# Attention and a mixture of experts on one core: late routing of one batch, a drain on GpSimd's queue, and one ScalarE copy moved forward

## The chip, the core and the metric

One core of a Trainium2 chip runs the whole program. Its engines are TensorE (PE), VectorE (DVE), ScalarE (ACT), GpSimd (POOL) and SyncE (SP), which only issues DMAs here. The metric is the device time of one execution in microseconds, as a median of several runs. PE does the matmuls; the other engines copy, split, rotate, reduce and issue transfers beside it.

## The reference, cut to what matters

The reference takes q, k, v of shape 8 x 8 x 576 x 64 (batch, heads, tokens, width) and computes an attention with rotary embedding, then a mixture of experts with one expert per token:

```python
q_rot, k_rot = rotate(q), rotate(k)
scores = q_rot @ k_rot^T / sqrt(64); attn = softmax(scores)
x = (attn @ v) as 4608 rows of 512                       # 8 batches of 576 rows
logits = x @ w_gate + modality_bias[modality_id]         # 8 experts
e = argmax(logits); gate = softmax(logits)[e]
out[rows of e] = gate * (relu(x[rows of e] @ w1[e]) @ w2[e])   # 512 -> 1024 -> 512
```

Which rows go to which expert is known only when the logits of all tokens are there, so the kernel has to sort rows by expert on the chip.

## The kernel before, in words

**Attention.** Two heads make a pair; there are 32 pairs, four for each batch of 576 tokens. Of every pair the program knows some sixty jobs by name: scores (S0 to S8), the row minimum on VectorE (MN), the exponential on ScalarE (EX), transposes of the probabilities (F0 to FB) with copies out of PSUM on ScalarE (A_) and VectorE (B_), the product with v (AV), the transposed output (OUT) with its scaling (EV). Rotary embedding of a pair that comes later runs on GpSimd (T1, T2, R, LO: `rope_`, lines 455 to 469) with one copy on ScalarE (HI); SyncE then swaps halves of the result by DMA (SWH, SWL, line 477) and loads q, k and v (LD, LD1, LV).

**Routing.** After the last pair of a batch (pairs 3, 7, 11, ...) fifteen steps RK0 to RK14 (`route`, line 646) find expert, gate and destination row of its 576 tokens. RK0 copies the logits of one half of the last 64 tokens (GpSimd), RK1 those of the other half (ScalarE, `tail1`), RK2 adds up the logits (VectorE), RK3 to RK7 find the best expert, RK8 (`ranks`) counts rows with small matmuls into a PSUM bank, RK9 (`runs`) takes the counts out and gives the bank back, RK10 to RK12 give the gate (into `VAL`), RK11, RK13 and RK14 the destination row. XO writes the batch's rows to a table X in DRAM, VO (`vout`, line 638) writes token number and gate beside them. BK0 to BK4 (`back`, line 752) read X back in five pieces through two buffers `XL`, taken in turn, and SC0 to SC4 (`scatter`, line 735) scatter each piece by an indirect DMA of GpSimd to the expert's region of a sorted table XS. VO and BK are issued by SyncE for batches 0 to 5 and by GpSimd for batches 6 and 7.

**Order.** Each job has a key in planner microseconds from its pair's start (KEYS, or EDGE[n] for a pair that has its own), plus 14.438 times the pair's number. All jobs are sorted by this key and issued so; every engine's queue keeps that order, and SyncE's too. A wait in a queue therefore holds everything behind it. PSUM slots are taken in the same order (`take`, `give`): one whose bank is held is passed over.

**Experts.** A first plan (`plan0`, on GpSimd with sums on VectorE) uses the rows of batches 0 to 4 alone: one block of 256 rows, then four of 512. Its tables wait for the scatters of those batches, and by declaration not for later ones. Batch 7 is routed between the products of the first blocks (`late`, `one`), and a second plan follows with four more blocks of 512, one of 256 and one of 128 rows. A block of 512 rows (`m_super`) multiplies the hidden layer with seven products of halves; `m_layer2` makes the second layer. Weights and rows are split into a high and a low part, by ScalarE and VectorE. `m_store` (line 1109) scales a 128-row tile on ScalarE into one of four buffers `sc` and scatters it to the output by an indirect DMA of GpSimd. The last two blocks (256 and 128 rows) run in `chain(NA + NSB, ns, True)`, line 1644; `m_half` stores the last one at line 1427. Behind it stands a branch for further blocks that isn't taken here, and then the program's end, in which every engine waits, drains and meets the others (these carry lines 1647 and 1746).

Of the kernel before, what the change touches and what calls it, by code (L numbers as in the profile page):

```python
# [19 lines left out]
B, H, S, D = 8, 8, 576, 64  # L20
# [29 lines left out]
    "B_F3": 13.72, "FA": 4.24, "A_FA": 6.1, "B_FA": 7.42, "FB": 11.93, "A_FB": 13.44, "B_FB": 13.66, "AVA": 11.22, "AVB": 16.42,  # L50
    "OTA": 12.47, "OTB": 19.33, "OUT": 24.24, "EVB": 26.37, "EVA": 25.82, "RE": 20.68, "RI": 25.25, "T1": -36.95, "T2": -32.1,
# [4 lines left out]
}  # L56
# [74 lines left out]
        "LD1": -42.214,  # L131
    },
    19: {
    },
    23: {
    },
    25: {
        "RE": 11.575, "F2": 13.246, "A_F2": 14.351, "B_F2": 14.486, "RI": 16.427, "AVB": 18.725, "OTB": 20.519, "OUT": 26.426,
# [92 lines left out]
def tile_attention_moe(ctx: ExitStack, tc: tile.TileContext, qk, v, mod, wg, mb, w1, w2, rope, cf, ci, out):  # L231
    nc = tc.nc
# [405 lines left out]
    def vout(b, eng=nc.sync):  # L638
        xd = X[b * S:(b + 1) * S, DM:XU]
        eng.dma_start(out=xd[0:512, :].rearrange("(p j) w -> p j w", j=4), in_=VAL[:, b, 0:4, :].bitcast(F32))  # L640
        eng.dma_start(out=xd[512:576, :], in_=VAL[0:64, b, 4, :].bitcast(F32))
# [93 lines left out]
    def scatter(b, j):  # L735
        oi = bt_[b]["oi"]
        n = P if j < 4 else 64
        inst = nc.gpsimd.indirect_dma_start(  # L738
            out=XS, out_offset=bass.IndirectOffsetOnAxis(ap=oi[0:n, j:j + 1], axis=0),
            in_=xl[b, j][0:n], in_offset=None, bounds_check=E * RS - 1, oob_is_err=False).ins  # L740

        for _b, x in placed:
            tc.declare_no_dep(inst, x, reason="rows of other tokens")
        placed.append((b, inst))
        if b >= NPL:
            for x in taken:
                tc.declare_no_dep(inst, x, reason="the first plan's blocks lie before the rows of later batches")
# [4 lines left out]
    def back(b, j, eng=nc.sync):  # L752
        t = xl[b, j] = XL[len(xl) % 2]
        xd = X[b * S:(b + 1) * S, 0:XU]
        if j < 4:
            eng.dma_start(out=t[:, 0:XU], in_=xd[0:512, :].rearrange("(p j) w -> j p w", j=4)[j])
        else:
            eng.dma_start(out=t[0:64, 0:XU], in_=xd[512:576, :])

    def pads():  # L760
        nc.vector.tensor_copy(CNT, RUN[0:1, B, :])
        for e in range(E):
            r = nc.sync.value_load(CNT[0:1, e:e + 1], min_val=0, max_val=E * RS - BLK)
            inst = nc.sync.dma_start(out=XS[bass.ds(r, BLK), 0:XU], in_=ZR[:, :]).ins
            for _b, x in placed:
                tc.declare_no_dep(inst, x, reason="rows behind those of the tokens")
            for x in taken:
                tc.declare_no_dep(inst, x, reason="the first plan's blocks are full")
            placed.append((B, inst))
# [250 lines left out]
    def m_rows(s, j=0):  # L1020
        d = ms[s]
        n = 4 * nt[s]
        if n == 4:
            ho = d["ho"] = ixp.tile([P, 2], I32, name="ho", tag="ho", bufs=1)
            for h in range(2):
                nc.gpsimd.tensor_scalar(ho[:, h:h + 1], d["ix"][:, 0, 0:1], 2.0, float(h), op0=ALU.mult, op1=ALU.add)
        rows = XS[bass.ds(d["r"], nt[s] * P), 0:DM].rearrange("(q r) (i f) -> i q r f", r=n, i=4)[:, :, 8 * j:8 * j + min(n, 8)]
        x = rows_of(s, j).rearrange("p t g f -> p (t g) f")[:, 0:min(n, 8)]
        for i in range(4):
            m_taken(s, nc.sync.dma_start(out=x[32 * i:32 * i + 32], in_=rows[i]).ins)  # L1030
# [26 lines left out]
    def m_split(i, g):  # L1057
        m_hi(i, g)
        m_lo(i, g)

    def m_tr(s, t, j=0):
        x = rows_of(s, j)[:, t]
        nc.vector.transpose(x, x)

    def m_tre(s, t, part=None):
        x = rows_of(s)[:, t].rearrange("p g (c q) -> p c g q", q=32)
        oh, ol = (a[:, :, t * P:(t + 1) * P].rearrange("p c (g q) -> p c g q", q=32) for a in (XTH, XTL))
        if part != 1:
            acopy(oh, x)
        if part != 0:  # L1070
            sub(ol, x, oh.bitcast(F32))
# [390 lines left out]
    def J(k_, nm, n, f, *a):  # L1462
        jobs.append((k_ + PER * n, len(jobs), f, a))
# [30 lines left out]
    for n in range(NPAIR):  # L1494
        def K_(nm, f, *a):
            J(EDGE.get(n, {}).get(nm, KEYS[nm]), nm, n, f, *a)

        for u in range(9):
            K_(f"S{u}", scores, n, u)
            K_(f"MN{u}", rowmin, n, u)  # L1500
            K_(f"EX{u}", expo, n, u)
        for f in ("F0", "F1", "F2", "F3", "FA", "FB"):
            K_(f, fill, n, f)
            for g in range(2):
                K_(f"{'AB'[g]}_{f}", evac, n, f, g)
        for w in range(2):
            c = "AB"[w]
            K_(f"AV{c}", AV, n, w)
            K_(f"OT{c}", avout, n, w)
            K_(f"EV{c}", ev, n, 1 - w)  # L1510
        K_("OUT", outp, n)
        for w in range(2):
            K_("R" + "EI"[w], rsum, n, w)
        if n > 0:
            for part, nm in ((1, "T1"), (0, "T2"), (2, "R"), (3, "HI"), (4, "LO")):
                K_(nm, rope_, n, part)
            for i in range(2):
                K_("SW" + "HL"[i], swap, n, i)
        K_("LV", loadv, n)
        if n > 2:  # L1520
            K_("LD1", load, n, 1)
            K_("LD", load, n, 0)
        if n % 4 == 3:
            K_("BIAS", bias, n // 4)
            K_("XO", xout, n // 4)
            steps = [(f,) for f in route(n // 4)]
            scats = [(scatter, n // 4, j) for j in range(5)]
            if n == z:

                planned = plan()  # L1530
                steps[0:2] = [(each, lambda f: f(), *steps[0:2])]
                late = steps + [(lambda: [vout(B - 1, nc.gpsimd)] + [(back(B - 1, j, nc.gpsimd), scatter(B - 1, j)) for j in range(5)] + [pads()],)] + [(each, next) + ((planned, None),) * 4] * 13
                continue
            for i, x in enumerate(steps):
                K_(f"RK{i}", *x)
            eng = nc.sync if n // 4 < B - 2 else nc.gpsimd
            K_("VO", vout, n // 4, eng)
            for i, x in enumerate(scats):
                K_(f"BK{i}", back, n // 4, i, eng)
                K_(f"SC{i}", *x)  # L1540
# [49 lines left out]
    def chain(lo, hi, begun):  # L1590
        if not begun:
            for g in range(4):
                m_split(0, g)
            for t in range(2):
                m_tr(lo, t)
                m_tre(lo, t)
        for s in range(lo, hi):
            nxt = s + 1 < hi
            half = nt[s] == 1
            if nxt:  # L1600
                if s + 2 < hi:
                    m_rows(s + 2)
                if s + 3 < hi:
                    m_plan(s + 3)
                    m_ix(s + 3)
                for g in range(4):
                    m_load1(s + 1, g)
            if half:
                m_half(s)
            else:  # L1610
                for g in range(4):
                    m_split(1, g)
                    m_l1(s, g)
                    m_l1e(s, g)
            if nxt:
                for g in range(2):
                    m_split(0, g)
                for t in halves(s + 1):
                    m_tr(s + 1, t)
                for t in halves(s + 1):  # L1620
                    m_tre(s + 1, t)
                for g in range(4):
                    m_load2(s + 1, g)
            last = nxt and nt[s + 1] == 1
            if not half:
                m_l2(s, 0)
            if last:
                for g in (2, 3):
                    m_split(0, g)
            if not half:  # L1630
                m_l2(s, 1)
            if nxt and not last:
                for g in (2, 3):
                    m_split(0, g)
# [6 lines left out]
    for s in range(2, NA + NSB):  # L1641
        m_super(s, s + 1)
    assert not late and next(planned, 0) == 0
    chain(NA + NSB, ns, True)
    order.close()
    tot = nc.values_load(TOT[0:1, 0:1], min_val=0, max_val=NB_MAX)
# [103 lines left out]
```

## Time and profile before

| what | value |
|---|---|
| time, median of 3 runs | 882.19 us (881.38 to 886.98) |
| the profiled execution | 884.29 us, span 882.5 us |
| PE busy | 833.9 us, 94% of the span |
| DVE, ACT, POOL busy | 708.9, 612.2, 453.5 us |
| granted PE clock, mean | 0.99 |
| DMA issued by software (GpSimd) | 7392 packets, 23.34 MB |

The span runs from the first to the last instruction of the program. PE is busy in nearly all of it; its busy time is modelled at the ends of matmuls, so a busy PE isn't one at its peak. The profile also lists sequencer steps (waits, branches, drains) under an engine's name with a q; they don't count as busy.

### The profile page before, as it was taken

What the parts mean: (1) busy time and instruction counts of PE and PEld (TensorE: products, weight loads), DVE (VectorE), ACT (ScalarE), POOL (GpSimd) and SP (SyncE); (2) the same over time, 40 slices, a digit from 0 to 9 for tenths busy, and PEclk for the clock granted to TensorE, in tenths of its full rate; (3) what the DMA queues carried; (4) which work ended last, traced back from release to release, by engine and by line L of the source; (5) the groups of instructions that cost most, each with busy time, mean ns of one, the idle gap of its engine ahead of it and who ended that gap; (6) DMA issues with size and microseconds to landing.
All of it is one profiled execution on the core that took longest, in us unless ns stands there. A gap on an engine that the chain in (4) does not pass through costs nothing.

```text
span 882.5 us, 24889 instructions
## 1 busy us (share of the span) xinstructions
PE 833.9 (94%) x9528; PEld 688.7 (78%) x9528; DVE 708.9 (80%) x1595; ACT 612.2 (69%) x1311; POOL 453.5 (51%) x365
## 2 busy tenths in 40 slices
PE   2899999999999999888999999999999999999992
PEld 2677777777777777676778989898989898989882
DVE  6888898888898888777888577989898998979360
ACT  2898989889888888777975446464656474748360
POOL 2999979989899898999511211024201112020100
PEclk9999999999999999999999999999999999999996
DMA  8877868979788797875877961377955413530520
GB/s 262 229 231 193 260 169 259 265 211 283 205 262 245 215 279 205 249 213 171 251 213 187 328 181 49 60 219 224 282 139 186 114 38 88 169 101 8 186 73 14
DMA packets 116330, 165.80 MB, mean 188 GB/s; under 512 B 31180, under 2 KB 76894, under 8 KB 116204
## 3 DMA queue, kind: packets, MB, share of 16 engines
q1 hardware_dynamic: 107468, 139.18, 55.2%
q0 software_dynamic: 7392, 23.34, 7.5%
q8 instruction: 77, 1.26, 0.6%
q10 hardware_dynamic: 1344, 1.62, 0.6%
q14 instruction: 49, 0.40, 0.1%
HBM read 118.14 MB, written 34.70 MB: 173 GB/s over the span
## 4 chain that ended last, share of the span: by engine, by line
PE 79%; DMA 5%; POOL 4%; ACT 4%; DVE 3%; issue 2%; SPq 1%; ACTq 0%; POOLq 0%; DVEq 0%
PE psY L1326 20%; PE ps L573 15%; PE psH L1202 14%; PE ps L492 13%; PE ps L515 9%; PE ps L608 2%; DMA SW<-HL 2%; PE psY L1202 2%; ACT P L510 1%; PE psH L1084 1%; PE psY L1103 1%; DMA ST<-in_rope_dram 1%; POOL HL L469 1%; DVE sc L501 1%; DMA ST<-in_moe_w_dram 1%
## 5 line engine op out<-in xcount | busy, mean ns | idle before, releaser
L501 DVE CUSTOM_DVE_ANT_1 sc<-ps,ZERO 128x576 f32<-128x576 f32 x288 | 206.6, 748 | 24.0 <-PE ps L492 11.3
L510 ACT ACTIVATE P<-sc,mn 128x576 f32<-128x576 f32 x256 | 195.5, 767 | 5.9 <-DVE mn L501 4.7
L492 PE MATMUL ps<-HL 64*128 64x288 f32 x960 | 167.9, 309 | 13.7 <-ACT HL L452 10.8
L492 PE MATMUL ps<-SW 64*128 64x288 f32 x960 | 168.1, 309 | 7.6 <-DMA SW<-HL 7.5
L1114 POOL DMA_INDIRECT out_dram<-sc,ix x36 | 43.4, 1206 | 222.1 <-ACT sc L1113 215.4
L492 PEld LDWEIGHTS ps<-HL 64*128 64x128 f32 x960 | 134.4, 188 | 19.5 <-ACT HL L452 10.8
L492 PEld LDWEIGHTS ps<-SW 64*128 64x128 f32 x960 | 134.3, 188 | 11.9 <-issue 9.4
L573 PE MATMUL ps<-PH,AT 128*64 128x320 f32 (+1 forms) x1024 | 139.6, 415 | 4.0 <-DVE PH L548 3.7
L1202 PE MATMUL psH<-HL,W1H 128*128 128x256 f32 x600 | 126.4, 279 | 0.4 <-ACT HL L452 0.4
L1202 PE MATMUL psH<-HL,W1L 128*128 128x256 f32 x400 | 111.6, 279 | 0.0
L573 PEld LDWEIGHTS ps<-PH,AT 128*64 128x64 f32 x1024 | 68.4, 137 | 53.1 <-DVE PH L548 7.0
L548 DVE COPY PH<-ps 128x512 f32<-128x512 f32 (+1 forms) x160 | 98.3, 630 | 11.0 <-PE ps L515 8.8
L452 ACT ACTIVATE PH<-ps 128x512 f32<-128x512 f32 (+1 forms) x160 | 85.3, 551 | 29.6 <-PE ps L515 26.0
L515 PEld LDWEIGHTS ps<-idf,P 64*128 64x128 f32 x2304 | 86.0, 138 | 20.7 <-ACT P L510 8.5
L1326 PE MATMUL psY<-W2L,SW 128*128 128x512 f32 x256 | 101.3, 396 | 0.0
L1326 PE MATMUL psY<-W2H,SW 128*128 128x512 f32 x256 | 100.9, 394 | 0.0
L515 PE MATMUL ps<-idf,P 64*128 64x64 f32 x2304 | 97.3, 225 | 2.8 <-ACT AT L452 1.7
L1202 PEld LDWEIGHTS psH<-HL,W1H 128*128 128x128 f32 x600 | 98.8, 188 | 1.1 <-ACT HL L452 0.6
L469 POOL TENSOR_TENSOR HL<-ST,HL 128x1152 fp32r<-128x1152 f32 x31 | 82.5, 2660 | 24.4 <-ACT HL L452 24.3
L465 POOL TENSOR_TENSOR ST<-ST 128x1152 f32<-128x1152 f32 x30 | 79.5, 2651 | 1.1
L738 POOL DMA_INDIRECT XS<-XL,oi x40 | 44.8, 1120 | 66.1 <-DMA XL<-X 45.2
L1202 PEld LDWEIGHTS psH<-HL,W1L 128*128 128x128 f32 x400 | 75.2, 188 | 0.0
(286 smaller groups left out, 1829.6 us busy)
## 6 DMA issues: line engine op xcount, KB each, us to landing
ST<-in_moe_w_dram SPq DMA_DIRECT2D x88, 512.0 KB
ST<-in_qk_dram SPq DMA_DIRECT2D x62, 576.0 KB
SW<-HL SPq DMA_DIRECT2D x124, 216.0 KB
AT<-in_v_dram SPq DMA_DIRECT2D x32, 256.0 KB
X<-X SPq DMA_DIRECT2D x8, 1024.0 KB
XL<-X SPq DMA_DIRECT2D x24, 257.0 KB
XG<-XS SPq DMA_DIRECT2D x40, 128.0 KB
XS<-ZR SPq DMA_DIRECT2D x8, 514.0 KB
```

The lines of the kernel that those rows point to most:

```text
L452: return nc.scalar.activation(o, i, AF.Copy, scale=scale)
L465: e.tensor_tensor(a, a, b, op=ALU.add)
L469: e.tensor_tensor(d["HL"][:, 1, o], a, d["HL"][:, 0, o].bitcast(F32), op=ALU.subtract)
L492: nc.tensor.matmul(ps[:, g, 0:288], t[:, wq, q0:q0 + P], t[:, wk, k0:k0 + 288], start=(m == 0), stop=(m == len(L) - 1))
L501: nc.vector.tensor_tensor_reduce(sc, d.pop(("S", u))[:, :, 0:288], ZERO.unsqueeze(2).to_broadcast([P, 2, 288]), 1.0, FMAX, ALU.add, ALU.mi ...
L510: nc.scalar.activation(p, sc.rearrange("p a b -> p (a b)"), AF.Exp, bias=mn, scale=-1.0, accum_out=d["sum"][:, u:u + 1])
L515: nc.tensor.transpose(ps[:, g, c:c + 64], src[r, k0:k0 + P], idf[r, r])
L548: alone(d["at", f], g, (nc.vector.tensor_copy if g else acopy)(o, i).ins, int(f[1] in "23B"))
L573: i = nc.tensor.matmul(pa[hh * 64:hh * 64 + 64, 0:c1 - c0], d["V"][:, hh, kt, :], r, start=(kt == 0), stop=(kt == 4))
L738: inst = nc.gpsimd.indirect_dma_start(out=XS, out_offset=bass.IndirectOffsetOnAxis(ap=oi[0:n, j:j + 1], axis=0), in_=xl[b, j][0:n], in_off ...
L1202: nc.tensor.matmul(ps[b][:, r * BLK:r * BLK + BLK], w[:, c, f0:f0 + P], x[:, c, :], start=(first and r == 0 and c == 0 and i == 0), stop=( ...
L1326: nc.tensor.matmul(po[t], hx[:, c, o:o + P], w[:, c, :], start=(k == 0 and c == 2 * q and i == 0), stop=(k == 3 and c == 2 * q + 1 and i = ...
```

## The change

Three things change. Of batch 5 (pair 23) the steps RK10 to RK14, VO, the five BK and the five SC get keys that put them behind the routing work of pairs 24 to 30 (VO from 69.0 to 129.3, for one), RK6 to RK9 move by up to 3.3, and VO and BK of this batch are issued by GpSimd. Of batch 4 (pair 19) three reads and three scatters swap places and come later. RK1 of every batch without a key of its own comes 1.53 earlier, which passes two exponentials of ScalarE. Last, a drain is put on GpSimd's queue between the last block of 512 rows and the last 256 and 128 rows.

```diff
-    "BIAS": 18.64, "RK0": 27.27, "RK1": 33.03, "RK2": 36.01, ...
+    "BIAS": 18.64, "RK0": 27.27, "RK1": 31.5, "RK2": 36.01, ...
     19: {
+        "BK0": 71.4, "BK1": 71.5, "BK3": 95.0, "BK2": 116.0, "BK4": 131.0,
+        "SC3": 113.825, "SC2": 128.215, "SC4": 152.075,
     },
     23: {
+        "VO": 129.3, "BK3": 130.0, "BK4": 130.1, "BK2": 132.5, "BK1": 133.0, "BK0": 137.0,
+        "RK6": 45.016, "RK7": 49.391, "RK8": 52.824, "RK9": 58.16, "RK10": 79.988, "RK11": 109.721, "RK12": 128.347, "RK13": 128.956,
+        "RK14": 129.684, "SC3": 130.859, "SC4": 132.359, "SC2": 132.942, "SC1": 136.961, "SC0": 137.506,
     },
...
-            eng = nc.sync if n // 4 < B - 2 else nc.gpsimd
+            eng = nc.sync if n // 4 < B - 3 else nc.gpsimd
             K_("VO", vout, n // 4, eng)
...
     assert not late and next(planned, 0) == 0
+    nc.gpsimd.drain()
     chain(NA + NSB, ns, True)
```

The keys that the two pairs had before are those of KEYS: RK6 48.27, RK7 49.58, RK8 55.05, RK9 55.78, RK10 58.29, RK11 62.64, RK12 64.05, RK13 67.72, RK14 74.22, VO 69.0, BK0 to BK4 71.4, 71.5, 90.0, 101.0, 114.0, SC0 to SC4 76.39, 91.58, 105.27, 118.91, 121.32.

## Rows read from the trace of the kernel before

**Rows 1.** The chain of waits: its shares by engine, and its last matmuls (start, us, what).

```profile
PE 79%; DMA 5%; POOL 4%; ACT 4%; DVE 3%; issue 2%; SPq 1%; ACTq 0%; POOLq 0%; DVEq 0%
...
861.41 3.00 PE psY L1422 x24
```

**Rows 2.** Waits of PE, 355 to 446 us: total, times, longest.

```profile
PE ps L573 <- DVE PH L548: 3.7, 2, 2.6
PE ps L515 <- ACT AT L452: 1.7, 1, 1.7
PE ps L492 <- DMA SW<-HL: 1.5, 1, 1.5
PE ps L701 <- DVE PH L548: 1.1, 1, 1.1
```

**Rows 3.** Stretches: length; PE, PEld, DVE, ACT, POOL busy; clock, DMA share, GB/s.

```profile
355.00:421.00 66.00, 57.78 (x940) 43.97 (x936) 50.55 (x153) 50.91 (x132) 60.30 (x71) 0.97 0.69 204
...
460.00:480.00 20.00, 20.00 (x220) 17.09 (x213) 17.21 (x32) 11.38 (x20) 1.42 (x2) 1.00 0.81 205
480.00:530.00 50.00, 49.29 (x307) 43.81 (x306) 34.78 (x49) 21.73 (x32) 10.68 (x13) 1.00 0.79 243
```

**Rows 4.** Timeline of POOL: its last scatter (start, us, instruction, idle before).

```profile
867.14 0.98 POOL L1427 DMA_INDIRECT out_dram<-sc,ho  x1 [0.44 <-issue]
```

**Rows 5.** DMA issues of POOL: count, size, median us from issue to landing.

```profile
XL<-X POOLq DMA_DIRECT2D x8, 257.0 KB, 5.5
...
out_dram<-sc,ix POOLq DMA_INDIRECT x36, 4.6
...
out_dram<-sc,ho POOLq DMA_INDIRECT x2, 3.0
...
XG<-in_moe_modality_id_dram POOLq DMA_DIRECT2D x1, 4.0 KB
```

**Rows 6.** Sequencer steps by line: count, ns min/median/max, first and last start.

```profile
L1746 POOLq DRAIN  x3: 46/109/8241, 873.4 to 882.2; - x3
L1746 SPq DRAIN  x3: 7/7/13, 874.1 to 881.9; - x3
...
L1647 POOLq INC_SWDGE_SEM  x1: 2200/2200/2200, 871.2 to 871.2; - x1
...
L1736 POOLq DRAIN  x1: 169/169/169, 0.3 to 0.3; - x1
```

**Rows 7.** Timeline of POOL: the first store of the last 256 rows.

```profile
848.35 0.98 POOL L1114 DMA_INDIRECT out_dram<-sc,ix  x1 [15.86 <-ACT sc L1113]
```

**Rows 8.** Timeline of ACT: a rotary copy and what it waited for.

```profile
414.99 1.16 ACT L452 ACTIVATE HL<-ST 128x1152 fp32r<-128x1152 f32 x1 [4.01 <-POOL ST L465]
```

**Rows 9.** Timeline of POOL: batch 5's first scatter.

```profile
411.18 1.10 POOL L738 DMA_INDIRECT XS<-XL,oi  x1 [0.29 <-POOL oi L728]
```

**Rows 10.** Waits of SP's queue, 380 to 446 us.

```profile
SPq L758 <- DMA XS<-XL,oi: 5.9, 1, 5.9
SPq L640 <- DVE pes L783: 4.9, 1, 4.9
```

**Rows 11.** Waits of DVE, 60 to 330 us.

```profile
DVE lg L669 <- ACT G L452: 4.8, 5, 1.0
```

**Rows 12.** Timeline of POOL: batch 6's table write, reads, a scatter, the store behind.

```profile
469.19 0.83 POOL L640 DMA_DIRECT2D X<-VAL  x1 [9.82 <-DVE VAL L721]
...
481.09 1.15 POOL L756 DMA_DIRECT2D XL<-X  x2 [0.44 <-issue]
...
488.09 1.02 POOL L738 DMA_INDIRECT XS<-XL,oi  x1 [0.30 <-issue]
...
513.78 0.98 POOL L1114 DMA_INDIRECT out_dram<-sc,ix  x1 [0.30 <-issue]
```

**Rows 13.** Timeline of ACT: the last store copy of the first 512 rows.

```profile
535.73 0.69 ACT L1113 ACTIVATE sc<-psY,ix 128x512 f32<-128x512 f32 x1 [0.70 <-issue]
```

**Rows 14.** Timeline of POOL: batch 7's slowest scatter.

```profile
602.77 2.65 POOL L738 DMA_INDIRECT XS<-XL,oi  x1 [7.28 <-DMA XL<-X]
```

2 rows, old and new, of the table KEYS are left out of this document.

## The prediction

> **What bounds the kernel now.** I read the chain of waits first: PE holds 79% of it, so the time is PE's own work plus the places where PE stands still or where something follows its last matmul [rows 1]. Then I listed what PE waited for between 355 and 446 us, the stretch in which batches 4 and 5 are routed: single waits of 0.9 to 2.6 us, each with a different releaser [rows 2]. From 446 us to the last matmuls PE waits for little. GpSimd is the tight engine up to 421 us (60.3 of 66 us busy) and nearly empty afterwards (1.4 of 20 us, then 10.7 of 50) [rows 3]. Last comes the end. PE is done by 864.4 us [rows 1]; the last scatter of GpSimd starts at 867.14 us [rows 4] and such a scatter lands 3.0 us after its issue [rows 5]. Still the span is 882.5 us. What fills the rest are two steps of GpSimd's queue: a semaphore step of 2.2 us at 871.2 and a drain of 8.24 us that starts at 873.4, when all of this has landed [rows 6]. SyncE is through its own waits at 874.1 [rows 6] and then stands until the drain ends.
>
> **The change, part by part.** Durations are of the profiled execution: 884.29 us for a span of 882.5. It is 2.1 us above the median of 882.19, so I take differences off the median.
>
> The drain. The trace has one long drain of GpSimd (8241 ns) and three short ones: 169 ns at the start, with no DMA issued yet, and 109 and 46 ns right behind the long one [rows 6]. So it isn't the instruction that is dear, and it isn't a wait for landings; it is something that piles up since the last drain and that a drain clears. What piles up on this queue are its DMAs: the fourteen rows of DMAs issued by GpSimd add up to 100 (the first, the last and two between are shown) [rows 5]. That is 8241 / 100 = 82 ns for one. The changed kernel has 107 (seven of batch 5 come over), 103 of them ahead of the new drain and 4 behind it: two stores of the 256 rows, two of the last 128. Price of the last drain then: 4 x 82 = 0.33 us. Lower bound of the gain: nothing, if a drain costs 8.24 us whenever any DMA lies behind it; upper bound: the whole 8.24, and 2.2 more if the semaphore step before it works off the same pile. I take the proportional one, because the two drains that directly follow the long one show that it leaves nothing. But the end then goes to SyncE, whose steps end at 874.1: 881.7 - 874.2 = **7.5 us gained**.
> The Trainium skill, VectorE: DVE Perf Modes, section "The DRAIN you can't avoid", says that the drains around a program take about 12 ns on every engine and always the same. By that neither drain would matter and this part would give 0; GpSimd's 8241 ns speaks against it.
>
> The new drain itself stands on GpSimd's queue behind the stores of the eighth 512-row block. The next work there is the store at 848.35, before which GpSimd sat idle for 15.86 us, waiting for ScalarE's copy [rows 7]. From 832.5, 3 to 5 us for the four stores to land [rows 5] and 8.5 us for 103 DMAs end at 846: inside. Nothing but those last four stores is queued behind it. Cost 0; without the cover it would push the store of 848.35, which has until the one of 867.14 before it shows.
>
> The later routing of batch 5. It takes from the stretch before 421 us five small steps (guard, own rank, gate, row sum, whole numbers) and the batch's first scatter; from SyncE's queue two table writes and five reads; from the stretch 421 to 456 four scatters. Term by term:
> - Ranks of batch 5 move two jobs forward on PE. There PE waited 1.1 us for a bank that VectorE's copy held [rows 2]. The new place needs a bank too, so between 0 and 1.1; I take 0.7. The bank is now held about 5 planner us instead of 0.7, since its sums come after two copies: against that I set up to 1.0 in the range.
> - PE's 1.7 us wait for ScalarE [rows 2] goes back to GpSimd: ScalarE stood 4.01 us for rotary work [rows 8] that began after batch 5's whole numbers and first scatter, 1.6 us together (1.10 of it the scatter) [rows 9]. Those go, but batch 4's third scatter (1.1 and its gap) comes into the same stretch. Net 0.4; bounds 0 and 1.7.
> - SyncE stood 5.9 us in front of batch 4's last read and 4.9 us in front of batch 5's table [rows 10]. Both go (the read comes 17 planner us later, the table moves to GpSimd). Swapped halves queued behind them land sooner, and the queues are less full at 441 us, where PE waited 1.5 us for one [rows 2]. I take half, 0.8; bounds 0 and 1.5.
> - The wait of 2.6 us at 361 us (inside the 3.7) [rows 2] goes back to the plan's sums, which nobody moves: 0.
> - Batch 4's other reads and scatters are only permuted: 0, hidden by the same queues. The first plan's tables need its last scatter, now at 426 on the planner's clock, 14 us ahead of their reading.
> - Price: 1.2 MB of reads and 1.2 MB of scatters of batch 5 now run between 463 and 500 us, where the DMA engines are 0.79 to 0.81 busy [rows 3]. W2 for the second block lands there. I take 0.4, bounds 0 and 2.
> Sum: 0.7 + 0.4 + 0.8 - 0.4 = **1.5 us gained**, bounds 4.3 gained and 3 lost.
>
> ScalarE's copy. VectorE's logits waited 4.8 us for it in five batches [rows 11], but PE had next to no waits there, so this hides behind PE: 0. For batch 5 it falls into ScalarE's idle time: 0.
>
> Sum: 7.5 + 1.5 = 9.0 us; 882.2 - 9.0 = **873.2 us**.
>
> **Rivals.**
> (1) A drain has a fixed price as soon as one DMA was issued since the last. For it: the trace holds no second long drain with few DMAs. Against it: only that 8.24 us is much for a mere check. Only the routing counts: 880.7 us.
> (2) The semaphore step shrinks as well. For it: it starts when the last landings are over and still takes 2.2 us [rows 6]; against it: nothing shows that it looks at older DMAs at all. 2.2 us more: 871.0 us.
> (3) GpSimd's queue gets too long: slower than before. Batch 5's gate is due at 460.4, where batch 6's, due at 468.8, released its table write at 469.19 [rows 12]. So batch 5's reads start near 463. Batch 6's chain, five reads and scatters through two buffers up to the store behind it, took from 481.09 to 513.78, 32.7 us [rows 12]. Batch 5 needs the same, so batch 6 starts near 499 and that store goes out near 532 instead of 513.78, landing 4.6 us later [rows 5], at 536. ScalarE wants its buffer at 535.73 [rows 13]. That is at the edge, and the first 2 or 3 us are ScalarE's to lose, as it is busy only 69% of the span. The rival decides from a store later than 534 on. The slowest row has a scatter of 2.65 us after a wait of 7.28 [rows 14], against 1.02 and 5.5 [rows 12, 5]: 3.4 us more for each of ten. At half that pace the store leaves at 549, ScalarE stands 18 us and PE 15: 873.2 + 15 = 888 us.
> The Trainium skill, SBUF — State Buffer, section "SBUF: two separate sides", has a rule for this: descriptors of GpSimd's DMAs can't be written while VectorE holds the port the two share, so such DMAs belong on SyncE. By that rule the seven DMAs that come over from SyncE stretch the chain, and the 2.65 us agree with it; the reads at 481 to 510 us don't show it (0.6 us each).
>
> **How the numbers follow.** Forecast 0.58, rival (1) 0.25, (2) 0.10, (3) 0.07. About 1% (8.8 us) is what a measurement of this kernel can tell from no change. The forecast lies on that edge; with its bounds (869 to 878) a little over half of it is faster by more, most of (2) as well: 0.32 + 0.08 = 0.40. Slower by over 1% is most of (3): 0.05. The rest, 0.55, is within. Range: 868 (between the best of the forecast and (2)) to 883 (rival (1) with 2 us lost in the routing); it leaves out (3) and the thin ends.
>
> **What would show it.** Right: a long GpSimd drain near 833 to 846 us and a last one under 1 us; no rows of PE waiting for the bank of the ranks; batch 5's scatters on GpSimd between 468 and 500; the store of the first 256 rows' second half near 530. Wrong: a last drain of 8 us again (rival 1); ScalarE waiting for a store's landing near 536 (rival 3); new PE waits of more than 2 us between 380 and 400, from the bank held longer.

## The result, and the profile after

The changed kernel takes 871.58 us in the median (869.71 to 876.84, 6 runs) beside 881.98 (880.35 to 888.66, 6 runs) of the kernel before; ratio 0.9872, 95% interval 0.9829 to 0.9915. Run once more beside the last experiments it gave 871.59 (ratio 0.9861, 0.9834 to 0.9889). So 10.4 us are gained by the first pair of medians and 12 by the second ratio, where 9.0 were forecast. The profiled execution took 869.71 us, span 867.9. Its span is 14.6 us shorter than that of the profiled one of before, more than the medians differ; a part of what the two profiles show is chance.

The gain lies in two stretches. The first is the attention's second half. PE's product for the output of a pair, listed by its line, first in a window around pair 23, then around pair 31 (count, ns min/median/max, first and last start); of before:

```profile
L608 PE MATMUL ps<-RW,AT x36: 222/223/273, 353.1 to 353.7; 64*64 64x72 f32 x36
L608 PE MATMUL ps<-RW,AT x36: 222/223/273, 477.4 to 478.0; 64*64 64x72 f32 x36
```

and of after:

```profile
L613 PE MATMUL ps<-RW,AT x36: 222/223/273, 353.1 to 353.8; 64*64 64x72 f32 x36
L613 PE MATMUL ps<-RW,AT x36: 222/223/273, 471.2 to 471.9; 64*64 64x72 f32 x36
```

Up to pair 23 nothing differs; the eight pairs behind take 118.1 us instead of 124.3. In the changed kernel these lines stand five further down (L608 is L613). What PE waited for from 355 to 446 us [rows 2], after:

```profile
PE ps L578 <- DVE PH L553: 2.8, 1, 2.8
PE ps L520 <- ACT AT L457: 1.4, 1, 1.4
PE ps L520 <- ACT P L515: 0.5, 1, 0.5
PE ps L520 <- issue: 0.3, 1, 0.3
```

The wait for the bank of the ranks and that for a swapped half are gone; the two that were largest are still there. The stretches [rows 3], after (the first one ends 4 us earlier, so that it holds the same 940 matmuls of PE):

```profile
355.00:417.00 62.00, 56.94 (x940) 43.91 (x936) 50.29 (x151) 50.49 (x132) 58.29 (x67) 1.00 0.68 203
...
454.00:474.00 20.00, 20.00 (x209) 17.05 (x202) 17.38 (x33) 10.81 (x18) 7.36 (x9) 1.00 0.85 220
474.00:524.00 50.00, 49.45 (x307) 43.97 (x306) 34.93 (x50) 22.23 (x32) 13.38 (x17) 1.00 0.85 255
```

PE's busy time for the same work fell by 0.8 us too: the granted clock was 1.00 where before had 0.97 [rows 3]. GpSimd has 2 us less to do there, and 6 and 3 us more in the two emptier stretches behind, where the DMA share is 0.85 and PE loses nothing.

The second stretch is the end. PE's last matmuls in the chain, after [rows 1]:

```profile
855.68 2.99 PE psY L1427 x24
```

The middle drain and the steps of the queues at the end, by line [rows 6], after (INC_SWDGE_SEM is the semaphore step):

```profile
L1649 POOLq DRAIN  x1: 7124/7124/7124, 825.5 to 825.5; - x1
...
L1653 POOLq INC_SWDGE_SEM  x1: 280/280/280, 866.0 to 866.0; - x1
...
L1752 POOLq DRAIN  x3: 46/109/380, 866.3 to 867.6; - x3
L1752 SPq DRAIN  x3: 7/7/13, 867.0 to 867.3; - x3
```

The last drain fell from 8241 to 380 ns, the semaphore step ahead of it from 2200 to 280. From the start of the last scatter [rows 4] to the end of the span there were 15.4 us, now 6.5. GpSimd's timeline around the middle drain [rows 7, 4], after:

```profile
827.02 1.53 POOL L1119 DMA_INDIRECT out_dram<-sc,ix  x1 [0.30 <-issue]
842.61 0.98 POOL L1119 DMA_INDIRECT out_dram<-sc,ix  x1 [14.05 <-ACT sc L1118]
...
861.40 0.98 POOL L1432 DMA_INDIRECT out_dram<-sc,ho  x1 [0.44 <-issue]
```

The drain ended at 832.6, 10 us before the next store was due.

### The profile page after: what moved, and what is told of

It is laid out like the page before. It is cut to its first block, busy times and chain, and to the rows that moved or that the text cites. A ratio compares the mean times of both kernels' runs of the same rounds, so it can differ in the third digit from the quotient of the medians.

```text
span 867.9 us, 24887 instructions
## 1 busy us (share of the span) xinstructions
PE 833.6 (96%) x9528; PEld 689.5 (79%) x9528; DVE 709.0 (82%) x1595; ACT 611.8 (70%) x1311; POOL 460.3 (53%) x372
## 4 chain that ended last, share of the span: by engine, by line
PE 46%; DVE 2%; POOL 1%; ACT 1%; issue 1%; SPq 1%; DMA 1%; POOLq 0%; ACTq 0%; DVEq 0%
PE psY L1331 20%; PE psH L1207 14%; PE ps L578 2%; PE psY L1207 2%; PE ps L520 1%; PE ps L497 1%; PE psH L1089 1%; PE psY L1108 1%; DMA ST<-in_moe_w_dram 1%; PE ps L1089 1%; PE psH L1403 1%; PE psY L1427 1%; DVE W2L L454 1%; SPq L1035 0%; PE ps L613 0%
## 5 line engine op out<-in xcount | busy, mean ns | idle before, releaser
L497 PE MATMUL ps<-HL 64*128 64x288 f32 x960 | 170.2, 312 | 12.5 <-ACT HL L457 11.3
L497 PE MATMUL ps<-SW 64*128 64x288 f32 x960 | 169.9, 312 | 4.2 <-DVE ST L468 3.6
L497 PEld LDWEIGHTS ps<-HL 64*128 64x128 f32 x960 | 136.3, 190 | 17.7 <-ACT HL L457 11.3
L497 PEld LDWEIGHTS ps<-SW 64*128 64x128 f32 x960 | 136.2, 190 | 8.8 <-DVE ST L468 3.9
```

The costliest lines, as they stand in the source:

```text
L497: nc.tensor.matmul(ps[:, g, 0:288], t[:, wq, q0:q0 + P], t[:, wk, k0:k0 + 288], start=(m == 0), stop=(m == len(L) - 1))
```

## The experiments

**The drain alone.**

```diff
 # the kernel before
     assert not late and next(planned, 0) == 0
+    nc.gpsimd.drain()
     chain(NA + NSB, ns, True)
```

> The kernel before, plus the drain on GpSimd's queue ahead of the last 256 rows; no routing step is moved. Theory (a last drain of GpSimd works off what was issued since the drain before it): the last drain falls from 8.24 us to under 0.5, the semaphore step ahead of it from 2.2 to about 0.3, as in the changed kernel; the time from PE's end to the span's end falls from 16.7 to about 7.9 us, and PE's last store is where it was (within 1 us of before). About 8.5 us faster: 873.5 us against 882, ratio 0.990. Rival (a drain has a fixed price, and the changed kernel's short end comes from batch 5's DMAs or from the order of the end): the last drain is 8 us again, and the time is that of before, 882. Rival (the tail is only part of it because the early drain pushes the stores behind it): the store of the first 128 of the 256 rows goes out later against PE's end than before, and less than 6 us are gained.

874.89 us beside 885.07, ratio 0.990 (0.9868 to 0.9932): 8.8 us by the ratio, 10.2 by the medians. Its steps:

```profile
L1644 POOLq DRAIN  x1: 9130/9130/9130, 831.6 to 831.6; - x1
...
L1648 POOLq INC_SWDGE_SEM  x1: 280/280/280, 871.2 to 871.2; - x1
L1747 POOLq DRAIN  x3: 46/109/380, 871.5 to 872.8; - x3
```

The rival of a fixed price falls: four DMAs behind the middle drain cost 380 ns. The early drain is hidden (it ends at 840.7, the next store starts at 848.68). Its attention is that of before. Its list of PE's waits from 355 to 446 us is the one to compare with that of the changed kernel above:

```profile
PE ps L573 <- DVE PH L548: 2.3, 1, 2.3
PE ps L515 <- ACT AT L452: 1.7, 1, 1.7
PE ps L492 <- DMA SW<-HL: 1.4, 1, 1.4
PE ps L492 <- ACT AT L452: 1.1, 1, 1.1
PE ps L701 <- DVE PH L548: 1.1, 1, 1.1
PE ps L608 <- DVE mn L501: 0.6, 1, 0.6
PE ps L573 <- DVE RUN L710: 0.3, 1, 0.3
```

**The routing alone.**

```diff
 # the changed kernel
-    nc.gpsimd.drain()
```

> The changed kernel without the drain: the late routing of batch 5, the swapped pieces of batch 4 and ScalarE's copy alone. Theory (the routing gains as much as the two traces differ in PE's progress from pair 23 to the end of the attention, 5.7 us): PE's last matmul 4 to 6 us earlier than before, the end as in the kernel before: semaphore step 2.2 us, last drain 8.2 to 8.8 us (107 DMAs by 82 ns: 8.8), so 876 to 878 us, ratio 0.994. Rival (the prediction's 1.5 us were right, and the rest of the 5.7 us is what two executions differ in): 880.5 us, ratio 0.998. Rival (the drain also helped the attention, which it can't unless executions overlap): time of before.

870.18 us, ratio 0.9854 (0.982 to 0.9889): as fast as the whole change (0.9872 and 0.9861), which none of the theories had. PE's gain is there (117.4 us for the eight pairs). But the end is short too, without any drain:

```profile
L1652 POOLq INC_SWDGE_SEM  x1: 480/480/480, 862.8 to 862.8; - x1
...
L1751 POOLq DRAIN  x3: 46/109/1217, 863.3 to 865.1; - x3
```

With 107 DMAs on the queue a drain of 8.8 us was expected. The experiments that follow look for the reason.

**The drain further forward**, right behind `m_plain(1, 2)`, with 44 DMAs behind it.

```diff
     m_plain(1, 2)
+    nc.gpsimd.drain()
     for s in range(2, NA + NSB):
         m_super(s, s + 1)
     assert not late and next(planned, 0) == 0
-    nc.gpsimd.drain()
```

> The changed kernel with its middle drain further forward: right behind the first of the eight 512-row blocks whose order isn't planned, so that 44 DMAs of GpSimd lie between it and the last drain instead of 4. Theory (price in proportion to the DMAs issued since the last drain, 82 ns each): last drain about 3.6 us, the semaphore step between 0.3 and 2.2 us, the end some 3 to 4 us later than in the changed kernel. Rival (one fixed price as soon as enough lies behind it): 8.2 us. Rival (any earlier drain will do, since the first one pays a price once): 0.4 us.

875.05 us, one run.

**Sixteen small DMAs behind the drain**, 20 in all:

```diff
     nc.gpsimd.drain()
+    for i in range(16):
+        nc.gpsimd.dma_start(out=SCR[i:i + 1, :], in_=EPS[0:1, :])
```

> The changed kernel with 16 more DMAs of GpSimd, of one element each, into a scratch table, right behind the middle drain: 20 DMAs lie between it and the last drain instead of 4, but hardly more bytes or packets. Theory (a price for each DMA, 82 ns): last drain 0.4 + 16 x 0.082 = 1.7 us. Rival (a price for each packet or byte; the 100 DMAs of before were 7392 packets, 8241 / 7392 = 1.1 ns for one): 0.4 us as in the changed kernel. Rival (fixed price above some number of DMAs): 0.4 or 8.2 us.

871.85 us, one run. The last steps of the two, first e3, then e4:

```profile
L1653 POOLq INC_SWDGE_SEM  x1: 1080/1080/1080, 867.6 to 867.6; - x1
...
L1752 POOLq DRAIN  x3: 46/109/3659, 868.8 to 873.0; - x3
```

```profile
L1656 POOLq INC_SWDGE_SEM  x1: 596/596/596, 866.5 to 866.5; - x1
...
L1755 POOLq DRAIN  x3: 109/194/1695, 867.1 to 869.6; - x3
```

Both are what the price per DMA gives (3.6 and 1.7 us). With 4, 20, 44 and 100 DMAs the drain takes 380, 1695, 3659 and 8241 ns: (8241 - 380) / 96 = 82 ns for each. The semaphore step takes 280, 596, 1080 and 2200: 20 ns for each. Size does not matter: a DMA of one element costs the same.

**Batch 5 alone**, with its new keys and GpSimd as issuer; batch 4's pieces and ScalarE's copy as before, no drain.

```diff
 # the kernel before
     23: {
+        "VO": 129.3, "BK3": 130.0, ... "SC0": 137.506,
     },
-            eng = nc.sync if n // 4 < B - 2 else nc.gpsimd
+            eng = nc.sync if n // 4 < B - 3 else nc.gpsimd
```

> The kernel before with batch 5's late routing alone (its new keys, and its table writes and reads issued by GpSimd): no swapped pieces of batch 4, ScalarE's copy where it was, no drain. 107 DMAs of GpSimd as in the changed kernel. Theory for the attention (batch 5's steps are what stood in the way between 370 and 446 us): PE gains 4.5 to 6 us from pair 23 to the last pair, as in the changed kernel without the drain (6.9 there, 6.2 with it). Rival (the swapped pieces of batch 4 and the earlier copy carry half of it): 2 to 3.5 us. For the end: run e2 had a last drain of 1.2 us with 107 DMAs and no middle drain, against 8.2 with 100. If the seven more DMAs do that, 1.2 us here too and about 871 us; if something else of the change does, 8.8 us and about 878.

870.61 us, ratio 0.9862 (0.9844 to 0.988): all of the gain. The eight pairs take 117.2 us and the last drain 1220 ns. So batch 4's swapped pieces and the copy add nothing that can be measured to it. What batch 4's pieces would do alone, no run shows.

**The same late steps, but issued by SyncE**, no drain.

```diff
 # the changed kernel
-            eng = nc.sync if n // 4 < B - 3 else nc.gpsimd
+            eng = nc.sync if n // 4 < B - 2 else nc.gpsimd
...
-    nc.gpsimd.drain()
```

> The changed kernel without its drain and with batch 5's table writes and reads left on SyncE (the same late keys): 100 DMAs of GpSimd, as before. Theory for the end (it is the number of GpSimd's DMAs that made e2's last drain short): 8.2 us again, 16 to 17 us from PE's end to the span's end. Rival (the late order does it): 1.2 us. For the attention: if it is the time of batch 5's steps that counts, the same 5.5 to 7 us from pair 23 on; if it is SyncE that is rid of seven DMAs, 2 us less. For the blocks behind: GpSimd's chain has seven DMAs less, so the store that left at 528.4 in the changed kernel leaves 3 to 6 us earlier and ScalarE's wait of 2.6 us for its landing is gone; rival: SyncE's reads stand for their two buffers and hold the weights queued behind them, and PE waits for these near 500 us. In all about 877 us.

890.74 us, ratio 1.0092 (1.0073 to 1.0112): slower than before. In its one trace the eight pairs take 119.3 us, among the 117.2 to 120.8 of the runs with the late steps on GpSimd (listed below), so it is the time of batch 5's steps that frees the attention, not the issuer. What is lost lies behind the attention: waits of SyncE's queue (440 to 515 us), ScalarE's timeline, waits of PE (470 to 515 us), in this order:

```profile
SPq L761 <- DMA XS<-XL,oi: 8.8, 3, 5.2
```

```profile
487.00 1.06 ACT L457 ACTIVATE W1H<-ST 128x1024 fp32r<-128x1024 f32 x1 [10.75 <-DMA ST<-in_moe_w_dram]
500.96 1.06 ACT L457 ACTIVATE W2H<-ST 128x1024 fp32r<-128x1024 f32 x1 [7.87 <-DMA ST<-in_moe_w_dram]
```

```profile
PE psH L1207 <- ACT HL L457: 5.0, 2, 2.7
```

SyncE's reads wait for their two buffers, the weights stand behind them in the same queue, ScalarE waits 10.75 and 7.87 us for these, and PE waits 5.0 us for ScalarE; from 490 to 500 us, behind PE's first stop, its granted clock is 0.74. This rival was right. For the end the theory held: 100 DMAs, 8241 ns and 2200 ns again.

**What shortens the end without a drain?** Three variants of the kernel before, each with more DMAs of GpSimd in the place of the drain: seven and twenty of one element (as in e4's diff), and the very seven that the change moves, issued once more.

```diff
 # the kernel before
     assert not late and next(planned, 0) == 0
+    vout(5, nc.gpsimd)
+    for j in range(5):
+        back(5, j, nc.gpsimd)
     chain(NA + NSB, ns, True)
```

> The kernel before with seven DMAs of GpSimd of one element each, into a scratch table, ahead of the last 256 rows, where the change has its drain: 107 DMAs in all, nothing else moved, no drain. Theory (at some number of DMAs between 100 and 107 the older ones are cleared without a drain): last drain near 1.2 us, span about 8 us shorter than before. Rival (it is bytes or packets, of which these seven bring hardly any, or the order): last drain 107 x 82 ns = 8.8 us and the time of before.

> The kernel before with batch 5's two table writes and five reads issued once more, by GpSimd, ahead of the last 256 rows: the very seven DMAs that the change moves to GpSimd, in size and shape, only late and to no use; no drain, nothing else moved. Theory (it is the volume of GpSimd's DMAs that clears older ones: 7616 packets don't, 7824 do): last drain 1.2 us or less, semaphore step 0.5 or less. Rival (it is when they are issued, in the middle of the program): 8.8 us and 2.3 us as with seven small ones.

> The kernel before with 20 DMAs of GpSimd of one element each ahead of the last 256 rows, no drain: 120 DMAs, some 8030 packets (seven such DMAs had brought 224), but no more bytes. Theory (packets): above 7824, so a short last drain, near 0.4 to 2 us. Rival (bytes, or descriptors of another count): 120 x 82 ns = 9.9 us, semaphore step 200 + 120 x 20 ns = 2.6 us.

883.77, 875.30 and 871.86 us, one run each. The page's row of GpSimd's queue (packets, MB, share) with the last drain, for seven small, the same seven, and twenty small:

```profile
q0 software_dynamic: 7616, 23.34, 7.5%
...
L1749 POOLq DRAIN  x3: 46/109/8812, 872.3 to 881.7; - x3
```

```profile
q0 software_dynamic: 7824, 24.53, 8.1%
...
L1749 POOLq DRAIN  x3: 51/109/1299, 871.1 to 873.0; - x3
```

```profile
q0 software_dynamic: 8032, 23.34, 7.7%
...
L1749 POOLq DRAIN  x3: 109/194/891, 867.8 to 869.6; - x3
```

Seven small ones only lengthen the drain, to 107 x 82 ns. The seven real ones shorten it although they come late, and twenty small ones shorten it although they bring no bytes. So it is neither their place nor bytes nor the number of DMAs (107 in the first two) alone. By the semaphore step (480, 500 and 400 ns; 200 and 20 for each DMA) 14 DMAs were left to the end in e2, 15 in f3 and 10 in f4; the older ones had been cleared without a drain.

The traces show where this happens. GpSimd's timeline: the second store of the last 512 rows in the kernel before and in e2, then a read in f3, then the second store of the last 256 rows in f4:

```profile
828.71 0.98 POOL L1114 DMA_INDIRECT out_dram<-sc,ix  x1 [0.38 <-ACT sc L1113]
```

```profile
822.11 0.99 POOL L1119 DMA_INDIRECT out_dram<-sc,ix  x1 [1.85 <-ACT sc L1118]
```

```profile
841.49 0.56 POOL L756 DMA_DIRECT2D XL<-X  x1 [6.36 <-issue]
```

```profile
851.94 1.30 POOL L1115 DMA_INDIRECT out_dram<-sc,ix  x1 [6.08 <-ACT W2H L453]
```

In the kernel before, the store starts 0.3 us after ScalarE's copy has ended. In e2 it starts 1.75 us after it, in f4 1.8 (f1, with seven small DMAs, has 0.3 there): GpSimd's queue is held 1.5 us. (In f3 the gap is 6.4 us; how much of it is the hold isn't shown.) At that store GpSimd stands 1.84 or 1.85 us in all seven traces that have batch 5 late and on GpSimd and no drain further forward (after twice, e2, e4, e5, the candidate below twice), and 0.37 to 0.39 us in before, e1, e3, e8n and f1; f3 and f4 have their hold later. From the held DMA on, 7 DMAs are issued in e2, 8 in f3 and 3 in f4; at the end 14, 15 and 10 were left. So in all three the same had been cleared: everything but the last seven DMAs ahead of the hold. This ties the clearing to the hold. It costs e2 nothing: two stores later GpSimd is idle for 14 us, and PE has no wait there. In e3 the forward drain has cleared the queue before, and there is no hold.

What sets it off stays open. Packets are not the measure: 7328 had been issued ahead of the hold in e2, 7280 in f3 and 7856 in f4, while f1 went to 7616 without one. The number of DMAs isn't either: the hold stands ahead of the 101st, the 100th and the 118th, and f1 issued 107.

**A candidate** from the stalls that are left: the first plan's sum 3.5 us later on VectorE, one rotary copy of ScalarE (pair 30) 0.55 us later, and batch 6's pieces after the first behind the store of the first block's second half.

```diff
 # the changed kernel
-    pl=(-114.356, -102.856, -99.906, -88.406, -85.506, ...),
+    pl=(-114.356, -102.856, -99.906, -88.406, -82.0, ...),
     30: {
-        ... "HI": -22.193, ...
+        ... "HI": -21.64, ...
+    # BK and SC of batch 6 behind the first SC: called behind m_l2(0, 1)
```

> A candidate: the changed kernel with three moves. The first plan's sum on VectorE 3.5 us later (VectorE and PE stood 2.8 us for it at 361 us); one rotary copy of ScalarE (pair 30) 0.55 us later, behind two jobs that it held up while waiting for GpSimd (PE 1.4 us at 411); and batch 6's reads and scatters after the first one behind the store of the second half of the first 256 rows on GpSimd's queue, so that this store leaves near 508 instead of 528 us. Theory: ScalarE's wait of 2.6 us for that store's landing at 529 goes, and with it most of PE's 1.1 us in front of batch 7's ranks at 543; 2.8 + 1.3 (the clock's dip behind it) + 1.4 + 0.6 = 6 us less than the changed kernel, 865.5. Rival (each wait is followed by the next one within a few us): under 2 us less, 870. Rival (the sum is late for the plan's tables, and the first block's rows come later): slower, PE waiting near 440 to 490.

> The changed kernel as it is, beside the candidate on the same chip. 871 to 872 us, ratio 0.987 as before.

> The candidate of run e11 once more, for a direct comparison with the changed kernel. By its trace the stall at 361 us is gone but came back behind it, so the progress of PE is that of the changed kernel: theory 870 to 871, within 0.3% of it. Rival (its median of 869.8 was real): 2 us faster, 0.998 of it or less.

869.82 us (ratio 0.9833, 0.9805 to 0.986) and, side by side with the changed kernel, 869.72 against 871.59 (0.9844, 0.982 to 0.9868, against 0.9861, 0.9834 to 0.9889). Its median is 1.8 us below that of the changed kernel both times, but the intervals overlap; that it is faster isn't shown. Its second trace, PE's longest waits from 355 to 446 us:

```profile
PE ps L520 <- ACT P L515: 0.9, 1, 0.9
PE ps L520 <- ACT AT L457: 0.8, 1, 0.8
```

The stall of 2.8 us at 361 us is gone, and six short ones stand in its place, 3.6 us in all where the changed kernel had 5.0. The rival (each wait is followed by the next) is nearer than the 6 us hoped for.

## Why the prediction was right, and where not

The time came out near the forecast, 871.58 us against 873.2, with both terms of the sum too small; it is nearer the 871.0 of rival (2), which had a chance of 0.10. The mechanism of the larger term, the drain, is real (e1). That the routing shortens the end as well, so that the drain isn't needed here, was not foreseen. It is luck that this second cause left the forecast standing: both remove the same cost.

**The drain term (7.5 us): price right, cause only half, size 1.4 us too small.** The price per DMA, 82 ns, holds to a few ns over five counts, and rival (1) fell with e1. Two things were missed. Rival (2) was true beside the forecast: the semaphore step fell by 1.9 us, and the end gained 8.9 us (15.4 to 6.5). The forecast let the end go to SyncE's steps and held these fixed. They start behind the semaphore step: 7.0 us after the start of the last scatter before (874.1 [rows 6, 4]), 5.6 after it now (867.0), which is the missing 1.4. And the drain isn't what did it in this kernel: e2 shows the same time without it. With the seven DMAs that the routing brings to GpSimd's queue, older ones are cleared anyway, ahead of the second store of the last 512 rows. I counted the seven (107) but took the pile to grow without end. The middle drain of the changed kernel shows it too: I set 8.5 us for 103 DMAs on top of the landing of the stores; it ended 4.1 us after the last store's issue was through (828.55 to 832.65). An estimate fits this: that store lands 4.6 us after its start [rows 5], at 831.6, and ten DMAs that are left take 0.8. In e1, where 96 DMAs had never been cleared, it was 7.9 us behind the last store (831.85 + 0.98, to 840.7), which is 96 x 82 ns. By the Trainium skill, VectorE: DVE Perf Modes, section "The DRAIN you can't avoid", e1 would have changed nothing; it gained 8.8 us.

**The routing term (1.5 us): direction right, size less than half.** Measured between pair 23 and pair 31: five traces with batch 5 where it was (before, e1, f1, f3, f4) take 120.5 to 124.3 us, 122.4 in the mean; six with it late and on GpSimd (after twice, e2 to e5) take 117.2 to 120.8, 118.4 in the mean. That is 4.0 us, where the two profiled executions differ by 6.2. The ratios say much the same: e5's 12.2 us less the 8.8 of e1 are 3.4. With the 8.9 of the end that makes 12 to 13 us, somewhat more than the 10.4 to 12 measured, so the routing's share is uncertain by some 2 us. By its steps:
- Ranks' bank, 0.7 set: 1.1 gone, and with it two waits around it that I gave no price, 1.1 for ScalarE and 0.3 for the counts in e1's list (0.9 and 0.3 in the trace of before). This is the largest error of the sum: I priced the one wait in [rows 2] that named the bank, and not its neighbours 2 us before and behind it. The one of 0.3 is for the counts that RK9 takes out of this bank; that the one for ScalarE hangs on the ranks too isn't shown.
- ScalarE's wait for GpSimd, 0.4 set: 1.7 became 1.4. ScalarE stood 4.01 us [rows 8] and still stands 3.31:

```profile
410.93 1.16 ACT L457 ACTIVATE HL<-ST 128x1152 fp32r<-128x1152 f32 x1 [3.31 <-POOL ST L470]
```

- Swapped halves, 0.8 set: all of the 1.5 gone, the upper bound. Of SyncE's waits of 5.9 and 4.9 us for batches 4 and 5 [rows 10] one of 0.5 is left. But this doesn't simply add up with the rest: in e5, without batch 4's swapped pieces, SyncE still waits 5.4 us in front of batch 4's read and PE 1.1 us for a swapped half, and its eight pairs take 117.2 us all the same.
- The plan's sum, 0 set: 2.6 and 2.8; right.
- Granted clock, not in the sum: 0.97 against 1.00 over that stretch [rows 3]. It is worth between 0.8 us (what PE's busy time differs by) and 2 us (3% of 66). That isn't the change's own. The second profile of the changed kernel has the same order of work, and behind a wait of PE of 2.0 us at 412 the clock is for a while at its lower level of 1.2 GHz, as this stretch shows (the clock is the third figure from the end):

```profile
414.00:422.00 8.00, 8.00 (x152) 7.24 (x154) 5.48 (x13) 6.66 (x20) 7.92 (x4) 0.79 0.59 162
```

That execution takes 120.8 us for the eight pairs instead of 118.1. In e1 a like dip (0.79) lay at 390 to 398 us, behind two waits of 1.1. So two traces of one kernel differ by 2.7 us here, and a single profile is no better than that.
- Price of the moved DMAs, 0.4 set: no wait of PE of over 0.4 us came of it between 446 and 540 us.

**ScalarE's copy, 0 set**: VectorE's waits for it [rows 11] are gone from the list, and e5 without the move is as fast. Right.

**Rival (3), GpSimd's chain.** The chain ran as worked out. Timeline of GpSimd, batch 5's first and last scatter, batch 6's table and last scatter, the store behind [rows 9, 12], after:

```profile
461.45 2.27 POOL L743 DMA_INDIRECT XS<-XL,oi  x1 [2.80 <-DMA XL<-X]
...
492.02 0.99 POOL L743 DMA_INDIRECT XS<-XL,oi  x1 [7.03 <-DMA XL<-X]
493.01 0.80 POOL L645 DMA_DIRECT2D X<-VAL  x1
...
526.70 1.44 POOL L743 DMA_INDIRECT XS<-XL,oi  x1 [1.33 <-DMA XL<-X]
528.44 1.00 POOL L1119 DMA_INDIRECT out_dram<-sc,ix  x1 [0.30 <-issue]
```

That is 528.4 for my 532. But the point from which it decides was wrong: I held 534 against a ScalarE that would want its buffer at 535.73 [rows 13]. With 6.3 us gained ahead of it ScalarE wants it at 529.4 (535.73 less 6.3), so it did wait; its timeline, after:

```profile
531.31 0.69 ACT L1118 ACTIVATE sc<-psY,ix 128x512 f32<-128x512 f32 x1 [2.62 <-DMA out_dram<-sc,ix]
```

Little of this reached PE: ahead of batch 7's ranks PE waited 0.5 us in the kernel before and 1.1 in the changed one (2.3 in e2). Nor is the store the only cause: in the candidate it leaves at 508 and 506, ScalarE's wait is gone, and PE still stands 0.9 to 1.1 there. The Trainium skill, SBUF — State Buffer, section "SBUF: two separate sides", would have these DMAs on SyncE; e8n did that and lost, for a reason of queue order. A slow scatter of 2.27 us is there, which fits the rule, though no row shows that VectorE caused it; it didn't decide.

## What to carry to other kernels

Two edits that remove the same cost don't add up, so run each alone before crediting either: here the drain, the edit with the clear mechanism, is worth 8.8 us alone and nothing that can be measured beside the other. A program's end can hold a bill for each DMA that GpSimd issued; look at the last drain and the step ahead of it, and count. When work moves to a later, emptier stretch, set every deadline there against the time that the change itself gains ahead of it, and choose the queue by what stands behind it: late reads on SyncE held up the weights, on GpSimd almost nothing.

## What the runs showed of the hardware that was not expected

- GpSimd's end costs 82 ns in the drain and 20 ns in the semaphore step for each of its DMAs that hasn't been cleared since the last drain, of any size (4 to 107 DMAs, 380 to 8812 ns).
- GpSimd's queue can be cleared without a drain. In e2, f3 and f4 everything but the last seven DMAs ahead of one point is cleared there, and the next DMA starts late: by 1.5 us in e2 and f4, behind a gap of 6.4 us in f3. Neither packets (7280 to 7856 ahead of that point, against 7616 in f1 without one) nor the number of DMAs (99 to 117, against 107) sets it off; what does stays open.
